# Agent attention and a gated feed-forward: TensorE's loop on 64-row tiles in pairs

## The chip, the cores and the metric

One core of a Trainium2 chip runs the whole problem in one launch. The metric is device time in microseconds (us). Engines are named as the profile names them: PE is TensorE (PEld its weight loads), DVE VectorE, ACT ScalarE, POOL GpSimd, SP SyncE. The L numbers are lines of the kernel before, unless said otherwise.

## The reference

```python
scale = 1.0 / np.sqrt(q.shape[-1])

def sm(a, b):
    s = scale * (a @ b.transpose(0, 2, 1))
    s = s - s.max(-1, keepdims=True)
    e = np.exp(s)
    return e / (e.sum(-1, keepdims=True) + 1e-09)
a2k = sm(agents, k)          # (4, 49, 12480)
agent_v = a2k @ v            # (4, 49, 128)
q2a = sm(q, agents)          # (4, 12480, 49)
x = (q2a @ agent_v).reshape(4 * 12480, 128)
h = x @ w_in                 # w_in 128 x 2048
g = h * (1.0 / (1.0 + np.exp(-1.702 * h)))
out = g @ w_out              # w_out 2048 x 128
```

All arrays are fp32 (w_in and w_out come as float64). There are 4 batches of 12480 tokens, 128 channels and 49 agents.

## The kernel before, in words

Tokens are taken in 52 row groups (13 per batch) of 960, in two halves of 480. F is 2048 wide, in 16 pieces of 128. The product of agent values and `w_in` is folded once per batch into weights of 49 rows, so that the first layer is `q2a` (49 rows by 480 tokens) against 49 x 128 weights. To keep fp32 accuracy with TensorE's rounded fp32 type (`fp32r`), each operand is split into a high and a low part, and a product is a sum of three: high by high, high by low, low by high.

The loop goes in steps of two pieces of F (`two_steps`, 416 of them). The *up* products (`up`, L442 and L445) give `ph`, a PSUM bank of 128 x 480 for each piece and half. The tiles `sa`, `sb` (128 rows) hold the high part, the low part and 30 rows of the third product together, and the 19 rows that are left come as four products on 32-row tiles of the array (`rq` by `wq`, one for each of four banks). ScalarE applies the GELU (`g`, L455). The high part `gh` of `g` is made by a transfer that POOL issues (`gh<-g`, L461), by ScalarE's cast (L465), or once per row group by VectorE; VectorE makes the low part `gl` (L470). The *down* products (L480) add into the two banks of `po`, LAG = 4 pieces behind: `wo_h` by `gh`, `wo_h` by `gl`, `wo_l` by `gh`, each of 128 rows and 480 columns, for either half. When all 16 pieces are in, ScalarE copies both banks out (`store`, L491). `po` has one buffer, `ph` has four.

Between these products lie the jobs of the attention, put at steps by a table (`at`): the query scores of a row group two ahead (48 products of 49 columns in bf16 in two runs, L202), their `Exp` on ScalarE with a table load ahead and one behind (L393), the transposes (L414), and, for the next batch, key scores (L202 too), keys' `Exp` (L285), value products (L300) and weights (L346). The order on PE, ACT, DVE and POOL is that of the code (`manual_schedule`); a queue works in that order.

Of the kernel before, what the change touches and what calls it, by code (L numbers as in the profile page):

```python
# [22 lines left out]
LAG = 4  # L23
G_BUFS = 5
GH_BUFS = 6
GL_BUFS = 4
PAD = 8
Q_AT = 12
E_AT = 0
P_AT = 4  # L30
S_AT = 8
K_AT = 3
V_AT = (6, 11)
V_LAST = 5
R = 30
FIRST_WORDS = 1
FIRST_UP = 2
BOTH = (0,)
ON_DVE = (2,)
# [4 lines left out]
def kernel(  # L44
# [28 lines left out]
    ps_m = ctx.enter_context(tc.tile_pool(name="ps_m", bufs=2, space=bass.MemoryType.PSUM))  # L73
# [11 lines left out]
    for c in range(2):  # L85
        nc.vector.tensor_add(
            out=sel[:, c * H : c * H + A], in0=ident[:, 0:A], in1=ident[:, H : H + A]
        )
        x = c * (R // 2)
        nc.vector.tensor_copy(out=sel[:, c * H + A : (c + 1) * H], in_=sel[:, x : x + R // 2])  # L90

    sel_q = const.tile([P, P], F32, name="sel_q")
    nc.vector.memset(sel_q, 0.0)
    nc.vector.tensor_copy(
        out=sel_q.rearrange("p (i x) -> p i x", i=4)[:, :, 0 : A - R],
        in_=sel[:, R:A].unsqueeze(1).broadcast_to([P, 4, A - R]),
    )

    twice = const.tile([P, 1], F32, name="twice")
    nc.vector.tensor_reduce(  # L100
        out=twice, in_=ident.rearrange("p (c x) -> p c x", c=2)[:, :, A:H], axis=AX.XY, op=ALU.add
    )
    nc.vector.tensor_scalar_mul(out=twice, in0=twice, scalar1=-1.0)
# [91 lines left out]
    def scores(b, parts, ps, c):  # L195
        x0, x1, x2 = parts
        for j in range(c * KB // 2, (c + 1) * KB // 2):
            t = slice(j * TB, j * TB + P)
            o = ps[:, j * A : (j + 1) * A]
            products = [(x0, 0), (x0, 1), (x0, 2), (x1, 0), (x1, 1), (x2, 0)]  # L200
            for i, (x, y) in enumerate(products):
                nc.tensor.matmul(  # L202
                    out=o,
                    lhsT=x[:, t],
                    rhs=ag_part[:, b, y, :],
                    start=(i == 0),
                    stop=(i == len(products) - 1),
                )

    def score_bank():  # L210
        ps = ps_m.tile([P, 512], F32, name="ps_m")
        return ps, ps[:TB, : KB * A].rearrange("p (j a) -> p j a", a=A)
# [7 lines left out]
    def first_key_scores(g, kt):  # L220

        for c in range(2):
            ps = ps_m.tile([P, 512], F32, name="ps_m")
# [11 lines left out]
        running_max(g, score[:TB, g * KB : (g + 1) * KB, :])  # L235

    def running_max(g, s):
        if g == 0:
            nc.vector.tensor_copy(out=run_max[:TB], in_=s)
        else:  # L240
            nc.vector.tensor_tensor(out=run_max[:TB], in0=s, in1=run_max[:TB], op=ALU.max)  # L241

    def key_store(g, s):
        nc.scalar.copy(out=score[:TB, g * KB : (g + 1) * KB, :], in_=s)  # L244
        running_max(g, s)
# [6 lines left out]
    def key_max_1(d):  # L252
        mx = d["mx"]
        ps = ps_m.tile([P, 512], F32, name="ps_m")
# [7 lines left out]
    def key_max_2(d):  # L262
        mrow = d["mrow"]
        ps = ps_m.tile([P, 512], F32, name="ps_m")
        nc.tensor.transpose(out=ps[:TB, :A], in_=mrow[:A], identity=ident[:A, :A])
        nc.vector.tensor_copy(out=max_b[:TB], in_=ps[:TB, :A])
# [31 lines left out]
    def key_matmuls(g, ps, first, last):  # L298
        for j in range(KB):
            nc.tensor.matmul(  # L300
                out=ps[:, : 2 * C + 2],
                lhsT=e_pair[g % 2][:TB, j, :],
                rhs=v_pair[:TB, j, :],
                start=(first and j == 0),
                stop=(last and j == KB - 1),
            )

    def key_values(g):
        ps = ps_m.tile([P, 512], F32, name="ps_m")
        key_matmuls(g, ps, True, True)  # L310
        return ps

    def key_sum(g, ps, acc):
        if g == 0:
            nc.vector.tensor_copy(out=acc, in_=ps[:, : 2 * C + 1])
        else:
            nc.vector.tensor_add(out=acc, in0=ps[:, : 2 * C + 1], in1=acc)


    def weights_0(acc, w):  # L320
        zc = work.tile([P, P], F32, name="zc", bufs=1)
        nc.vector.tensor_copy(out=zc, in_=acc[:, 2 * C : 2 * C + 1].broadcast_to([P, P]))
        w["acc"], w["zc"] = acc, zc

    def weights_1(w, to=sel, name="avT"):
        ps = ps_m.tile([P, 512], F32, name="ps_m")
        nc.tensor.matmul(out=ps[:, 0:P], lhsT=w["acc"][:, 0:C], rhs=to, start=True, stop=False)
        nc.tensor.matmul(out=ps[:, 0:P], lhsT=w["acc"][:, C : 2 * C], rhs=to, start=False, stop=True)
        nc.tensor.matmul(out=ps[:, P : 2 * P], lhsT=w["zc"], rhs=to, start=True, stop=True)
# [3 lines left out]
        avT = work.tile([P, P], F32, name=name, bufs=1)  # L333
        nc.vector.tensor_mul(out=avT, in0=ps[:, 0:P], in1=rz)
        w[name] = avT

    def weights_part(b, w, c):  # L340
        if c == 0:
            wts[b] = wpool.tile([P, F], F32R, name="wh"), wpool.tile([P, F], F32R, name="wq")
        wh, wq = wts[b]
        s = slice(c * 512, (c + 1) * 512)
        pw = ps_m.tile([P, 512], F32, name="ps_m")
        nc.tensor.matmul(out=pw, lhsT=w["avT"], rhs=w_in_sb[:, s], start=True, stop=True)  # L346
        nc.scalar.copy(out=wh[:, s], in_=pw)
        wl = work.tile([P, 512], F32R, name="wl")
        nc.vector.tensor_sub(out=wl[:A], in0=pw[:A], in1=wh[:A, s].bitcast(F32))
        move(wh[A:H, s], wl[0 : R // 2])  # L350
        move(wh[H + A : P, s], wl[R // 2 : R])
        for i in range(4):
            move(wq[i * 32 : i * 32 + A - R, s], wl[R:A])


    def weights_direct(b, w, c):
        if c == 0:
            wts[b] = wpool.tile([P, F], F32R, name="wh"), wpool.tile([P, F], F32R, name="wq")
        wh, wq = wts[b]
        s = slice(c * 512, (c + 1) * 512)  # L360
        pw = ps_m.tile([P, 512], F32, name="ps_m")
        nc.tensor.matmul(out=pw, lhsT=w["avT"], rhs=w_in_sb[:, s], start=True, stop=True)
        hi = work.tile([P, 512], F32R, name="wl")
        nc.scalar.copy(out=hi, in_=pw)
        nc.vector.scalar_tensor_tensor(  # L365
            out=wh[:, s], in0=hi.bitcast(F32), scalar=twice, in1=pw, op0=ALU.mult, op1=ALU.add
        )
        pq = ps_m.tile([P, 512], F32, name="ps_m")
        nc.tensor.matmul(out=pq, lhsT=w["avQ"], rhs=w_in_sb[:, s], start=True, stop=True)
        hi = work.tile([P, 512], F32R, name="wl")  # L370
        nc.scalar.copy(out=hi, in_=pq)
        nc.vector.tensor_sub(out=wq[:, s], in0=pq, in1=hi.bitcast(F32))

    def move(out, in_):
        nc.sync.dma_start(out=out.bitcast(F32), in_=in_.bitcast(F32))
# [7 lines left out]
    def query_shift(s):  # L383
        m = work.tile([P, KB], F32, name="m")
        nc.vector.tensor_reduce(out=m[:TB], in_=s, axis=AX.X, op=ALU.max)
        sd = e_sb[:TB, :, 0:A]
        nc.vector.tensor_tensor(
            out=sd, in0=s, in1=m[:TB].unsqueeze(2).broadcast_to([TB, KB, A]), op=ALU.subtract
# [21 lines left out]
    def query_pairs(g):  # L410
        pp = p_pad
        ps = ps_m.tile([P, 512], F32, name="ps_m")
        for i in range(CH // TB):
            nc.tensor.transpose(  # L414
                out=ps[:, i * TB : (i + 1) * TB], in_=pp[:TB, i, :], identity=ident[:TB, :TB]
            )
        sa = work.tile([P, CH], F32R, name="sa")
        sb = work.tile([P, CH], F32R, name="sb")
        rq = work.tile([P, CH], F32R, name="rq")
        hi = sa[0:A], sb[H : H + A]  # L420
        lo = sa[H : H + A], sb[0:A]
        parts = ps[0:A, :CH], ps[H : H + A, :CH]
        for c in range(2):
            nc.scalar.copy(out=hi[c], in_=parts[c])
        for c, t in enumerate((sa, sb)):
            nc.vector.tensor_sub(out=lo[c], in0=parts[c], in1=hi[c].bitcast(F32))
            move(t[A:H], hi[c][0 : R // 2])
            move(t[H + A : P], hi[c][R // 2 : R])
            for i in (c, c + 2):
                move(rq[i * 32 : i * 32 + A - R], hi[c][R:A])  # L430
        return sa, sb, rq
# [3 lines left out]
    def up(f, wts, pairs):  # L435
        wh, wq = wts
        rq = pairs[2]
        tiles = [(i, c) for i in range(2) for c in range(2)]
        cols = [slice((f + i) * P, (f + i + 1) * P) for i in range(2)]
        ph = [ps_h.tile([P, 512], F32, name="ph") for _ in tiles]  # L440
        for k, (i, c) in enumerate(tiles):
            nc.tensor.matmul(out=ph[k][:, :CH], lhsT=wh[:, cols[i]], rhs=pairs[c], start=True, stop=False)  # L442
        for k, (i, c) in enumerate(tiles):
            r = slice(k * 32, k * 32 + A - R)
            nc.tensor.matmul(  # L445
                out=ph[k][:, :CH],
                lhsT=wq[r, cols[i]],
# [386 lines left out]
```

## Time and profile before

| | us |
|---|---|
| runs, median (lowest to highest of 3) | 2044.2 (2042.5 to 2045.38) |
| span of the profiled execution, first to last instruction | 2042.8 |
| PE busy | 1992.6 |
| DVE busy | 1581.9 |
| ACT busy | 1445.3 |
| POOL busy | 279.2 |

The span is that of one execution under the profiler; its own time isn't listed apart from the runs, the lowest of which lies 0.3 under the span and the highest 2.6 over it. Busy time is the union of an engine's instructions. A product counts as busy to its modelled end, so products that start 0.22 us apart and take 0.38 each leave no idle time; starts say more than ends. In a timeline "x2" on a row merges instructions of one kind that follow each other, and the number in brackets is idle time before the row with what ended it.

### The profile page before, as it was taken

Reading aid. Unit: us, or ns where it says so; the run is one execution under the profiler, and the core shown is the slowest. Engines: PE = TensorE matmul, PEld = TensorE weight load, DVE = VectorE, ACT = ScalarE, POOL = GpSimd, SP = SyncE. Lnnn points to the kernel's source line nnn. Section 1 sums busy time; section 2 is a strip of 40 time slices with the busy share of each in tenths; the row PEclk is TensorE's granted clock in tenths of the full one; section 3 lists DMA queues with packets and bytes.
Section 4 is the critical chain, followed back from the end, with each engine's and each line's share of the span. In section 5 each row is a group of like instructions: output and inputs, shape, how many; then the busy total and the mean of one; then the engine's idle time right before and its main releaser. Section 6 shows DMA issues by size and latency. Waiting matters only on the chain.

```text
span 2042.8 us, 36429 instructions
## 1 busy us (share of the span) xinstructions
PE 1992.6 (98%) x13702; PEld 1524.1 (75%) x13702; DVE 1581.9 (77%) x2038; ACT 1445.3 (71%) x2463; POOL 279.2 (14%) x590
## 2 busy tenths in 40 slices
PE   8779999999999999999999999999999999999999
PEld 7457777777777777777777777777777777777777
DVE  5678888888677879978777878888877776767665
ACT  3357667777776677677676677777777777777775
POOL 3011111111111111111111111111111111111111
PEclk9789999999999999999999999999999999999999
DMA  9545556656455555565555556566545545445443
GB/s 253 155 151 173 178 172 189 177 179 192 157 173 172 185 184 179 179 188 175 171 174 169 181 189 183 172 190 174 170 164 158 179 153 174 156 167 168 161 156 135
DMA packets 128836, 355.13 MB, mean 174 GB/s; under 512 B 15476, under 2 KB 48468, under 8 KB 128660
## 3 DMA queue, kind: packets, MB, share of 16 engines
q0 software_dynamic: 67392, 230.06, 34.5%
q1 hardware_dynamic: 61268, 122.75, 20.8%
q8 instruction: 108, 1.77, 0.4%
q14 instruction: 68, 0.56, 0.1%
HBM read 80.97 MB, written 25.56 MB: 52 GB/s over the span
## 4 chain that ended last, share of the span: by engine, by line
PE 88%; DVE 6%; issue 2%; ACT 2%; DMA 2%; SPq 0%; POOL 0%; ACTq 0%; POOLq 0%; DVEq 0%
PE po L480 52%; PE ph L442 17%; PE ph L445 8%; PE ps_m L202 5%; PE ps_m L300 2%; DVE gl L470 1%; PE ps_m L414 1%; PE ps_m L225 1%; ACT g L455 1%; DVE rest L191 1%; DVE rest L189 1%; DMA gh<-g 1%; PE po L622 1%; PE ps_m L346 0%; DMA words<-w_in 0%
## 5 line engine op out<-in xcount | busy, mean ns | idle before, releaser
L455 ACT ACTIVATE g<-ph 128x480 f32<-128x480 f32 x1664 | 816.8, 577 | 491.3 <-PE ph L445 485.2
L470 DVE TENSOR_TENSOR gl<-g,gh 128x960 fp32r<-128x960 f32 x832 | 941.7, 1153 | 194.8 <-DMA gh<-g 104.7
L480 PE MATMUL po<-gh,wo_h 128*128 128x480 f32 x1664 | 550.7, 412 | 0.0
L480 PE MATMUL po<-gl,wo_h 128*128 128x480 f32 x1664 | 500.8, 382 | 5.3 <-DVE gl L470 4.6
L480 PE MATMUL po<-gh,wo_l 128*128 128x480 f32 x1664 | 499.1, 381 | 0.0
L461 POOL DMA_DIRECT2D gh<-g x468 | 252.1, 539 | 1720.8 <-ACT g L455 1224.5
L480 PEld LDWEIGHTS po<-gl,wo_h 128*128 128x128 f32 x1664 | 310.7, 188 | 63.5 <-DVE gl L470 15.7
L480 PEld LDWEIGHTS po<-gh,wo_l 128*128 128x128 f32 x1664 | 313.1, 188 | 49.6
L480 PEld LDWEIGHTS po<-gh,wo_h 128*128 128x128 f32 x1664 | 272.8, 189 | 82.9 <-issue 64.8
L442 PE MATMUL ph<-sb,wh 128*128 128x480 f32 x832 | 321.1, 386 | 3.2 <-ACT g L455 3.2
L442 PE MATMUL ph<-sa,wh 128*128 128x480 f32 x832 | 319.6, 384 | 2.3 <-DVE wh L365 1.5
L465 ACT CAST gh<-g 128x960 fp32r<-128x960 f32 x312 | 311.7, 999 | 9.0
L445 PE MATMUL ph<-rq,wq 19*128 19x480 f32 x1664 | 204.2, 480 | 0.0
L442 PEld LDWEIGHTS ph<-sb,wh 128*128 128x128 f32 x832 | 156.9, 189 | 38.9 <-ACT g L455 14.8
L442 PEld LDWEIGHTS ph<-sa,wh 128*128 128x128 f32 x832 | 156.8, 189 | 35.2 <-ACT g L455 7.2
L445 PEld LDWEIGHTS ph<-rq,wq 19*128 19x128 f32 x1664 | 79.6, 181 | 136.1 <-issue 136.1
L202 PE MATMUL ps_m<-ag_part,rest 128*128 128x49 bf16 x2184 | 130.4, 184 | 7.8 <-DVE rest L191 7.7
L191 DVE TENSOR_TENSOR rest<-rest 128x480 bf16<-128x480 f32 (+1 forms) x182 | 129.8, 719 | 0.4
L202 PEld LDWEIGHTS <-rest 128*128 128x128 bf16 x2184 | 109.4, 97 | 9.8 <-DVE rest L191 9.4
L241 DVE TENSOR_TENSOR run_max<-ps_m,run_max 120x392 f32<-120x392 f32 x36 | 20.4, 567 | 79.3 <-ACT score L244 79.2
L202 PEld LDWEIGHTS <-qt 128*128 128x128 bf16 x1248 | 61.0, 97 | 24.6 <-issue 24.5
L202 PE MATMUL ps_m<-ag_part,qt 128*128 128x49 bf16 x1248 | 74.3, 186 | 0.0
(116 smaller groups left out, 1345.5 us busy)
## 6 DMA issues: line engine op xcount, KB each, us to landing
gh<-g POOLq DMA_DIRECT2D x468, 480.0 KB, 3.4
kt<-kT SPq DMA_DIRECT2D x52, 480.0 KB
qt<-qT SPq DMA_DIRECT2D x52, 480.0 KB
vt<-v SPq DMA_DIRECT2D x52, 480.0 KB
outT<-o SPq DMA_DIRECT2D x104, 240.0 KB
rq<-sa SPq DMA_DIRECT2D x104, 35.6 KB
rq<-sb SPq DMA_DIRECT2D x104, 35.6 KB
sa<-sa SPq DMA_DIRECT2D x104, 28.1 KB
```

What stands on the lines that cost most here:

```text
L189: nc.vector.tensor_sub(out=r[:, s], in0=t[:, s], in1=halves(t)[0][:, s])
L191: nc.vector.tensor_sub(out=halves(r)[1][:, s], in0=r[:, s], in1=halves(r)[0][:, s])
L202: nc.tensor.matmul(out=o, lhsT=x[:, t], rhs=ag_part[:, b, y, :], start=(i == 0), stop=(i == len(products) - 1),)
L225: nc.tensor.matmul(out=ps[:TB, j * 2 * A : (j + 1) * 2 * A], lhsT=kt[:, c * KB // 2 + j, :], rhs=ag_sb[:, 0:2, :].rearrange("p b a -> p (b ...
L300: nc.tensor.matmul(out=ps[:, : 2 * C + 2], lhsT=e_pair[g % 2][:TB, j, :], rhs=v_pair[:TB, j, :], start=(first and j == 0), stop=(last and ...
L442: nc.tensor.matmul(out=ph[k][:, :CH], lhsT=wh[:, cols[i]], rhs=pairs[c], start=True, stop=False)
L445: nc.tensor.matmul(out=ph[k][:, :CH], lhsT=wq[r, cols[i]], rhs=rq[r], start=False, stop=True, tile_position=(k * 32, 0),)
L455: nc.scalar.activation(out=gs[i][:, c, :], in_=ph[k][:, :CH], func=AF.Gelu_apprx_sigmoid)
L461: nc.gpsimd.dma_start(out=gh, in_=g)
L465: nc.scalar.copy(out=gh, in_=g)
L470: nc.vector.tensor_sub(out=gl, in0=g, in1=gh.bitcast(F32))
L480: nc.tensor.matmul(out=po[c][:, :CH], lhsT=lhsT[:, f, :], rhs=rhs[:, c, :], start=(begin and first), stop=(end and last),)
```

## The change

All products of the loop go onto tiles of 64 rows of the array, in pairs: two products, one on rows 0 to 63 and one on rows 64 to 127, stand next to each other and write different banks.

- *Up*: for one piece of F, three pairs (`wh` by `q_hi`, `wh` by `q_lo`, `wl` by `q_hi`), the upper rows for one half of the tokens and the lower for the other. `sa`, `sb`, `rq`, `wq` and the small transfers that filled their spare rows go; `q_hi`, `q_lo`, `wl` come.
- *Down*: the 128 rows of a piece are two sets of 64. In a first half each row tile adds its rows into one bank of `po` (three pairs), in a second half the row tiles have changed banks (three more pairs). Where the row tile that writes a bank changes, the first product waits for a relay: a `nop` in POOL's queue that itself waits for a product of TensorE that stands behind the bank's last one. The up products of another piece lie between the halves.
- *Order*: the loop goes in gaps (`gap`), 17 for a row group, one with no up products. A gap has jobs, an up step of one piece, the second half of a piece and the first half of the next. LAG is 6. Transfers for `gh` are issued one gap late, at the gap's end; pieces 1 and 9 go by transfer too, and none by VectorE.
- *Scores, value products and transposes* are cut into 64-row pairs as well. The buffers of `ps_m` are one pair of banks in place of two banks. Products with `avT`, and the keys' maximum, stay on 128 rows.
- *Store*: ScalarE copies one bank, VectorE the other.

```diff
-LAG = 4
+LAG = 6
 G_BUFS = 5
-GH_BUFS = 6
-GL_BUFS = 4
+GH_BUFS = 7
+GL_BUFS = 5
...
+    def half_matmul(key, c, **kw):
+        ins = nc.tensor.matmul(tile_position=(c * H, 0), **kw)
+        last = writers.get(key)
+        if last is not None and last[0] != c:
+            while rests[0][0] <= last[1]:
+                rests.pop(0)
+            n, ended, relay = rests[0]
+            if relay is None:
+                relay = rests[0][2] = nc.gpsimd.nop()
+                tc.add_manual_dep(relay.ins, ended.ins.name, behind, reason="bank")
+            tc.add_manual_dep(ins.ins, relay.ins.name, behind, reason="bank")
...
     def up(f, wts, pairs):
-        wh, wq = wts
-        rq = pairs[2]
-        tiles = [(i, c) for i in range(2) for c in range(2)]
-        cols = [slice((f + i) * P, (f + i + 1) * P) for i in range(2)]
-        ph = [ps_h.tile([P, 512], F32, name="ph") for _ in tiles]
-        for k, (i, c) in enumerate(tiles):
-            nc.tensor.matmul(out=ph[k][:, :CH], lhsT=wh[:, cols[i]], rhs=pairs[c], start=True, stop=False)
...
+        products = [(wh, q_hi), (wh, q_lo), (wl, q_hi)]
+        for k, (w, q) in enumerate(products):
+            for c in range(2):
+                r = slice(c * H, c * H + A)
+                half_matmul(
+                    ph[c].name,
+                    c,
+                    out=ph[c][:, :CH],
+                    lhsT=w[r, cols],
+                    rhs=q[r],
...
+    def down(f, gh, gl, po, swap, begin, end):
+        products = [(wo_h, gh), (wo_h, gl), (wo_l, gh)]
+        for i, (w, x) in enumerate(products):
+            for c in range(2):
+                to = c ^ swap
+                r = slice(c * H, (c + 1) * H)
+                half_matmul(
+                    po[to].name,
...
     def store(b, g, po):
         for c in range(2):
             o = work.tile([P, CH], F32, name="o", tag="o")
-            nc.scalar.copy(out=o, in_=po[c][:, :CH])
+            if c == 0:
+                nc.scalar.copy(out=o, in_=po[c][:, :CH])
+            else:
+                nc.vector.tensor_copy(out=o, in_=po[c][:, :CH])
...
+        before, late[:] = list(late), []
+        rest()
         for job in at.pop(t, ()):
             job()
...
+        if u is not None:
+            if u < steps:
+                do_up(u)
+                rest()
+            do_low(u - 3)
         if t >= LAG:
...
+            do_downs(n, k)
+        for u in before:
+            do_high(u)
+
+    def do_downs(n, k):
+        if k == 0:
+            po[n] = [ps_o.tile([P, 512], F32, name=f"po{c}") for c in range(2)]
+        first_whole = NF - LAG - 1 if n == B * NG - 1 else NF
+        if 0 < k <= first_whole:
+            do_down(n, k - 1, True)
+        if k < first_whole:
+            do_down(n, k, False)
+        elif k < NF:
+            do_down_whole(n, k)
+        else:
+            store(*divmod(n, NG), po.pop(n))
```

The order of instructions shows it at three places. First TensorE in the middle of a row group; this is one step before (in brackets what an instruction waits for):

```order
L442 MATMUL ph<-sa,wh 128x480 [waits Activation_49]
L442 MATMUL ph<-sb,wh 128x480 [waits Activation_49]
L442 MATMUL ph<-sa,wh 128x480 [waits Activation_49]
L442 MATMUL ph<-sb,wh 128x480 [waits Activation_49]
L445 MATMUL ph<-rq,wq 128x480 x4
L480 MATMUL po_12946<-gh,wo_h 128x480
L480 MATMUL po_12947<-gh,wo_h 128x480
L480 MATMUL po_12946<-gl,wo_h 128x480 [waits DVE_49]
L480 MATMUL po_12947<-gl,wo_h 128x480
L480 MATMUL po_12946<-gh,wo_l 128x480
L480 MATMUL po_12947<-gh,wo_l 128x480
```

And this is TensorE in one gap of the change (lines of the changed kernel; `Pool_sequencer` is the relay):

```order
L192 MATMUL ph<-q_hi,wh 128x480 [waits Activation_49] x2
L192 MATMUL ph<-q_lo,wh 128x480 x2
L192 MATMUL ph<-q_hi,wl 128x480 x2
L192 MATMUL po_13879<-gh,wo_h 128x480 [waits Pool_sequencer_49]
L192 MATMUL po_13878<-gh,wo_h 128x480
L192 MATMUL po_13879<-gl,wo_h 128x480
L192 MATMUL po_13878<-gl,wo_h 128x480
L192 MATMUL po_13879<-gh,wo_l 128x480
L192 MATMUL po_13878<-gh,wo_l 128x480
L192 MATMUL po_13879<-gh,wo_h 128x480
L192 MATMUL po_13878<-gh,wo_h 128x480
L192 MATMUL po_13879<-gl,wo_h 128x480 [waits DVE_49]
```

The four-fold 32-row products are gone, an up step has six products of one piece, and the second half of a piece (its first row waits for the relay) is followed by the first half of the next. There are 915 such waits in the program, 825 of them at down products.

The second place is ScalarE from the end of a row group to the `Exp` of the next, before:

```order
L393 ACT_TABLE_LOAD
L393 ACTIVATE e_sb<-e_sb 120x8x49
L455 ACT_TABLE_LOAD
L455 ACTIVATE g<-ph 128x480 x4
L491 COPY o<-po_6721 128x480
L491 COPY o<-po_6722 128x480
L455 ACTIVATE g<-ph 128x480 x4
L424 CAST sa<-ps_m 49x480
```

And in the change:

```order
L480 ACTIVATE g<-ph 128x480 x4
L491 CAST gh<-g 128x960
L526 COPY o<-po_2682 128x480
L480 ACTIVATE g<-ph 128x480 x4
L491 CAST gh<-g 128x960
L480 ACTIVATE g<-ph 128x480 x2
L406 ACT_TABLE_LOAD
L406 ACTIVATE e_sb<-e_sb 120x8x49
L480 ACT_TABLE_LOAD
L480 ACTIVATE g<-ph 128x480 x4
```

The `Exp` and its tables have moved from ahead of the copies to behind them, four gaps into the row group, and the copy now stands behind a cast of `gh`.

The third place is TensorE at the first down products of a row group, before:

```order
L414 MATMUL ps_m<-ident,p_pad 128x120 [waits DVE_49,PE_49]
L414 MATMUL ps_m<-ident,p_pad 128x120 x3
L480 MATMUL po_3205<-gh,wo_h 128x480 [waits DMASW4_49,Activation_49]
L480 MATMUL po_3206<-gh,wo_h 128x480 [waits Activation_49]
L480 MATMUL po_3205<-gl,wo_h 128x480 [waits DVE_49]
```

And in the change, where the run of 24 score pairs and one up step stand ahead of them:

```order
L192 LDWEIGHTS rest
L192 MATMUL ps_m<-ag_part,rest 128x49
L192 MATMUL ph<-q_hi,wh 128x480 [waits Activation_49] x2
L192 MATMUL ph<-q_lo,wh 128x480 x2
L192 MATMUL ph<-q_hi,wl 128x480 x2
L192 MATMUL po_14583<-gh,wo_h 128x480 [waits DMASW4_49,Activation_49]
L192 MATMUL po_14584<-gh,wo_h 128x480 [waits DVE_49]
L192 MATMUL po_14583<-gl,wo_h 128x480
```

Either bank now waits for its own copy, on ScalarE or on VectorE, and what stands ahead of the wait is other work.

## Rows read from the trace of the kernel before

**Rows 1.** The page: busy time and shares, and the chain that ended last.

```profile
PE 1992.6 (98%) x13702; PEld 1524.1 (75%) x13702; DVE 1581.9 (77%) x2038; ACT 1445.3 (71%) x2463; POOL 279.2 (14%) x590
...
PE 88%; DVE 6%; issue 2%; ACT 2%; DMA 2%; SPq 0%; POOL 0%; ACTq 0%; POOLq 0%; DVEq 0%
```

**Rows 2.** Windows by stretch: busy us of each engine, granted clock, DMA.

```profile
core 0: us, PE busy (x) PEld busy (x) DVE busy (x) ACT busy (x) POOL busy (x), PEclk, DMA share, GB/s
...
800.00:1200.00 400.00, 397.46 (x2716) 302.04 (x2715) 324.07 (x418) 291.99 (x496) 52.59 (x114) 1.00 0.57 179
```

**Rows 3.** Waits of TensorE's weight loads: us in total, times, longest.

```profile
PEld ph L445 <- issue: 136.1, 415, 0.4
PEld po L480 <- issue: 64.8, 279, 0.5
PEld L202 <- issue: 42.9, 179, 0.4
PEld ph L442 <- ACT g L455: 22.0, 68, 3.5
PEld po L480 <- DVE gl L470: 15.7, 35, 3.5
```

**Rows 4.** Timeline, one step and the quiet end: start us, us.

```profile
999.77 0.38 PE L442 MATMUL ph<-sb,wh 128*128 128x480 f32 x1
...
1003.64 0.39 PE L442 MATMUL ph<-sa,wh 128*128 128x480 f32 x1
1003.64 0.19 PEld L442 LDWEIGHTS ph<-sb,wh 128*128 128x128 f32 x1
1003.87 0.38 PE L442 MATMUL ph<-sb,wh 128*128 128x480 f32 x1
...
1004.31 0.38 PE L442 MATMUL ph<-sb,wh 128*128 128x480 f32 x1
1004.61 0.19 PEld L445 LDWEIGHTS ph<-rq,wq 19*128 19x128 f32 x4 [0.33 <-issue]
1004.61 0.49 PE L445 MATMUL ph<-rq,wq 19*128 19x480 f32 x4
1005.03 0.30 PEld L480 LDWEIGHTS po<-gh,wo_h 128*128 128x128 f32 x2 [0.23 <-issue]
1005.03 0.70 PE L480 MATMUL po<-gh,wo_h 128*128 128x480 f32 x2
1005.13 1.03 ACT L455 ACTIVATE g<-ph 128x480 f32<-128x480 f32 x2 [1.10 <-PE ph L445]
1005.36 0.40 PEld L480 LDWEIGHTS po<-gl,wo_h 128*128 128x128 f32 x2
...
2033.23 0.60 PE L480 MATMUL po<-gh,wo_h 128*128 128x480 f32 x2
2033.67 0.60 PE L480 MATMUL po<-gl,wo_h 128*128 128x480 f32 x2
```

**Rows 5.** Timeline, a run of 24 score products and the down products behind.

```profile
1010.11 0.25 PE L202 MATMUL ps_m<-ag_part,qt 128*128 128x49 bf16 x3
...
1010.73 0.68 PE L480 MATMUL po<-gh,wo_h 128*128 128x480 f32 x2
...
1011.25 0.59 PE L480 MATMUL po<-gl,wo_h 128*128 128x480 f32 x2
```

**Rows 6.** Timeline of ScalarE: a cast, the exponentials and the store.

```profile
1007.12 1.00 ACT L465 CAST gh<-g 128x960 fp32r<-128x960 f32 x1
...
1021.72 1.28 ACT L393 ACT_TABLE_LOAD   x1
...
1023.45 0.51 ACT L285 ACTIVATE score<-score 120x392 f32<-120x392 f32 x1
1023.99 1.28 ACT L455 ACT_TABLE_LOAD   x1
1025.28 1.96 ACT L455 ACTIVATE g<-ph 128x480 f32<-128x480 f32 x4
1027.10 1.05 ACT L491 COPY o<-po 128x480 f32<-128x480 f32 x2
```

**Rows 7.** Timeline of POOL: the issue of a transfer.

```profile
1006.46 0.53 POOL L461 DMA_DIRECT2D gh<-g  x1 [3.57 <-DVE gl L470]
```

**Rows 8.** Groups by line: products of the second set of weights.

```profile
L369 PE MATMUL ps_m<-w_in_sb,avQ 128*128 128x512 f32 x8 | 6.3, 886 | 0.0
```

More of the change, by code (lines that the diff above doesn't have):

```diff
@@ L88 @@
         )
[L89 to L103, printed above, removed]
     e_pair = []
@@ L332, in weights_1, with weights_parts @@
         nc.vector.reciprocal(out=rz, in_=rz)
-        avT = work.tile([P, P], F32, name=name, bufs=1)
+        avT = work.tile([P, P], F32, name="avT", bufs=1)
         nc.vector.tensor_mul(out=avT, in0=ps[:, 0:P], in1=rz)
-        w[name] = avT
-    def weights_part(b, w, c):
+        w["avT"] = avT
+    def weights_parts(b, w, c):
         if c == 0:
[L342 to L353, printed above, removed]
@@ L356, in weights_direct @@
[L356 to L372, printed above, removed]
@@ new lines, in query_pairs @@
+        ps = two_banks()
+        q_hi = work.tile([P, CH], F32R, name="q_hi")
+        q_lo = work.tile([P, CH], F32R, name="q_lo")
+        r = slice(0, H + A)
+        rows = [slice(0, H), slice(H, TB)]
+        for i in range(CH // TB):
+            for c, t in enumerate(rows):
+                n = t.stop - t.start
+                half_matmul(
+                    (ps.name, c),
+                    c,
+                    out=ps[:, c, i * n : (i + 1) * n],
+                    lhsT=pp[t, i, :],
+                    rhs=ident[t, t],
+                    start=True,
+                    stop=True,
+                    is_transpose=True,
+                )
@@ new lines, in piece, with scored @@
+        def piece(q, c):
+            t = rows[c]
+            return q[r].rearrange("p (i t) -> p i t", t=TB)[:, :, t]
+        def scored(c):
+            n = rows[c].stop - rows[c].start
+            return ps[r, c, : CH // TB * n].rearrange("p (i t) -> p i t", t=n)
+        for c in range(2):
+            nc.scalar.copy(out=piece(q_hi, c), in_=scored(c))
+        for c in range(2):
+            nc.vector.tensor_sub(out=piece(q_lo, c), in0=scored(c), in1=piece(q_hi, c).bitcast(F32))
+        return q_hi, q_lo
@@ L507 @@
     pairs = {}
+    exps = {}
     def do_key_load(b, g):
@@ L639 @@
     weights_1(w0)
-    weights_1(w0, sel_q, "avQ")
-    for c in range(2):
-        if c:
-            up_weights(c, words_in[c])
-        weights_direct(0, w0, c)
-    for i in range(4):
-        do_query_split(1, i)
-    ahead(1)
-    do_query_softmax(1)
+    up_weights(1, words_in[1])
+    weights_parts(0, w0, 0)
     down_weights(0, words[0])
     steps = B * NG * NF
-    per_batch = NG * NF
+    gaps = LAG + B * NG * GAPS
     at = {}
-    pe_steps = {n * NF + f for n in range(B * NG) for f in (Q_AT, Q_AT + 1, P_AT)}
+    busy = set()
@@ L657, in put, with gap_of, take, free @@
+    def gap_of(u):
+        if u < LAG:
+            return u
+        n, k = divmod(u - LAG, NF)
+        return LAG + n * GAPS + (k + 1 if k else 0)
     def put(t, fn):
         at.setdefault(t, []).append(fn)
-    def pe_step(t):
-        while t in pe_steps:
+    def take(t, runs):
+        assert not busy.intersection(range(t, t + runs)), t
+        busy.update(range(t, t + runs + 1))
+    def free(t):
+        while t in busy or t + 1 in busy:
             t += 1
-        pe_steps.add(t)
+        take(t, 1)
@@ L738, with do_high, do_up, do_low @@
     po = {}
-    def jobs(t):
+    late = []
+    def do_high(u):
+        gh[u] = high(u % NF, g[u])
+    def do_up(u):
+        n, f = divmod(u, NF)
+        g[u] = up(f, wts[n // NG], pairs[n])
+        if by_dma(f):
+            late.append(u)
+        else:
+            do_high(u)
+        if f == NF - 1:
+            pairs.pop(n)
+    def do_low(u):
+        if 0 <= u < steps:
+            gl[u] = low(g.pop(u), gh[u])
+    def do_down(n, f, second):
+        u = n * NF + f
+        down(f, gh[u], gl[u], po[n], (f + second) % 2, f == 0 and not second, f == NF - 1 and second)
+        if second:
+            gh.pop(u), gl.pop(u)
@@ L792 @@
     with tc.manual_schedule(engines={E.PE, E.Activation, E.DVE, E.Pool}):
-        for t in range(0, steps + LAG, 2):
-            two_steps(t)
-    assert not at
+        for t in range(gaps):
+            gap(t)
+    assert not at, sorted(at)
 _INS = ["qT", "kT", "v", "agT", "w_in", "w_out"]
```

399 lines of the change are left out of this document (196 added, 203 removed).

## The prediction

> **What bounds the kernel now.** I read the shares of busy time first: TensorE is busy 98% of the span, and the chain that ended last lies on it for 88% [rows 1]. That alone doesn't say that its products are the limit, since a product counts as busy until its modelled end. So next the stretches: from 800 to 1200 us TensorE is busy nearly throughout at a granted clock of 1.00 (2.4 GHz), VectorE for 324 of 400 us and ScalarE for 292 [rows 2]. Both have room, VectorE not much. Then the waits: the longest on TensorE's weight loads have no releaser ("issue"): 136.1 us ahead of the 19-row products, 64.8 ahead of the first product for `po`, 42.9 ahead of the scores; next to them 22.0 for ScalarE's GELU and 15.7 for VectorE's low part [rows 3]. The timeline shows what "issue" is. The four up products start some 0.22 apart; then nothing starts for 0.30 us, until four 19-row loads and products start together (1004.31 to 1004.61); the next 128-row product starts 0.42 later, and its load stands open before the second one goes (1005.03 to 1005.36) [rows 4]. These are the passages from 128-row to 32-row tiles and back. They cost TensorE idle time in every step, so the stage is bound by TensorE with two drains in it.
>
> **The change, part by part.** All sums go against the span of 2042.8 us; the runs' median, 2044.2, is 1.4 above it.
>
> *Up products.* A step of two groups of F takes 4.10 us from one second up product to the next (999.77 to 1003.87) and holds 16 full products besides the 19-row four [rows 4]. The new step holds no passage: 3 pairs up and 6 pairs down for each group, 18 pairs in two. What a pair of 64-row products takes is in no row. Nearest are the full products, 0.22 apart (two in 0.44 even at the end, where other engines are idle), and the four 19-row ones, which start together [rows 4]. So I take one pair for one product, 0.218: 3.92 us, 0.18 less, times 416 steps: **-75 us**. Bounds: 480 columns at 2.4 GHz are 0.200, with 0.003 between starts 0.203, so 7488 pairs could take 112 us less still; weights that load one tile after the other (0.11 each, below) would make a pair 0.222, 30 more.
>
> *Scores.* Before, a run of 24 score products takes 0.62 us (1010.11 to 1010.73) [rows 5]; now 24 pairs. As pairs they cost the same; one after the other 0.62 more per run, 113 us for the 182 runs of 91 groups. The 19-row four start together, so I stand near the low end, +0.1 per run for loads that wait in order: **+18**. Behind a run the load of the first full product is open (0.52 for two products, 1010.73 to 1011.25, in place of 0.44) [rows 5]. Before, one of the two runs stood where a drain had just been paid; now both runs, and the transposes too, stand between 480-column products: 143 x 0.085 = **+12**.
>
> *The store.* `po` has one buffer, so the first down product of a row group waits until both copies of the group before are done. On ScalarE the copy now stands behind the GELU of that gap and the cast of `gh` behind it. I count from the gap's start: the third up pair starts at 0.44 and ends at 0.82 (0.38 long), the GELU starts 0.03 later and takes 1.03 [rows 4], the cast 1.00 and the copy 0.55 [rows 6]: 3.5. TensorE has up (0.65) and the second half (0.65), then in the next gap scores (0.71) and up (0.65): 2.66. So it waits 0.84, where before both copies followed straight on the GELU (1027.10 to 1028.15 [rows 6]) and no wait for them is among the long ones [rows 3]. 51 x 0.84 = **+43**. Bounds: nothing, if scores slower than pairs fill the time; 0.9 per group. VectorE's copy of the other half is done earlier by the same count.
>
> *The exponentials.* Two table loads and the query's `Exp` take 3.05 us (1021.72 to 1025.28, less the 0.51 for the keys) [rows 6]. They now stand ahead of a single GELU whose `ph` buffers are wanted two gaps, 3.92 us, later, and whose transfer's issue stands in POOL's queue ahead of a relay. GELU ends at 3.05 + 1.03 = 4.08: `up` waits 0.2. Issue starts 0.30 after the GELU and takes 0.53 (1006.16, 1006.46) [rows 4, 7], so the relay behind it runs at about 5.0, while TensorE comes to its wait at 4.77: 0.25 more. In 21 of the 51 groups the keys' `Exp` adds about 0.8: 1.3 in all. 30 x 0.45 + 21 x 1.3 = 41; of the 22.0 that is there now [rows 3] nothing else is left, so **+19**. Bounds: -22 to +40.
>
> *The relay elsewhere.* Queued behind its wait on TensorE are the second half's six products and all that follows. The product that it waits for ends 0.38 after its start; POOL and TensorE answer in 0.03 to 0.30 each (1005.10 to 1005.13 on ScalarE, 0.30 at POOL) [rows 4, 7]: 0.44 to 0.98. The last pair's own 0.22 and three up pairs, 0.65, hide 0.87. The upper end is a transfer's preparation, which a relay doesn't need; I take it as hidden: **0**. Without the up products it would cost 0.2 to 0.7 per gap.
>
> *Smaller parts.* The keys' maximum and the weights still run on 128 rows: 15 places with a passage either way, 0.4 each: **+6**. The start loses the second set of weight products (6.3 us of TensorE for `avQ` [rows 8]), but VectorE still converts the same words: **-6**, between -12 and 0. A lag of six groups in place of four should spare part of VectorE's 15.7: **-8**, between -15 and +10, as VectorE keeps its work in a shorter time.
>
> Sum: -75 + 18 + 12 + 43 + 19 + 6 - 6 - 8 = +9, or **2052 us**: the drains that go are given back in waits on ScalarE.
>
> A rule that bears on the pairs: the Trainium skill, "TensorE: Matmul & The Clock Gate", Part 3, § The mechanism, says that a weight load overlaps a running product only where its row group differs. The rows show otherwise: a 128-row load starts with the product on the same rows (both at 1003.64) and the next product follows 0.23 later [rows 4]. By the rule each tile's next load would stand open; what that gives is a rival below.
>
> **The rivals.** *A pair is faster than a full product.* It decides soon: 9 us over 7488 pairs is 1.2 ns, so below some 0.217 per pair the sum is under the time before. Toward 0.203 to 0.212 it gives 1940 to 2010. For it: nothing shows that the 0.018 beyond 480 columns belongs to 64-row tiles. Against: the same 0.22 in the quiet end [rows 4] speaks for a pace of the operand's stream, not of a neighbour.
>
> *The new waits don't come.* If ScalarE is far enough ahead, store and exponentials give 62 us less: 1990. For it: ScalarE is idle 27% of the time [rows 2]. Against: it works in order, and the chain of GELU, cast and copy starts only when its up products end.
>
> *Scores one by one.* +95 on the sum, less some 31 that fall into the wait for the store: 2115. For it: two instructions with a load per 49 columns; against: the 19-row four.
>
> *The relay shows in every gap.* If POOL and TensorE take 0.2 more than hidden, 832 x 0.2 = 166: 2220. It decides from an answer over 0.49 in all. For it: POOL's 0.30; against: that is a transfer's.
>
> *Loads open in each tile.* A first load after a drain takes some 0.11 (1005.03 to the second product's turn; four of them overlap) [rows 4]; 7488 x 0.11 = 800: 2850. Against: the load at 1003.64. It is the case that the Trainium skill's rule, cited above from "TensorE: Matmul & The Clock Gate", would have.
>
> **How the numbers follow.** Given back, 2025 to 2085: 0.48 (of it 0.10 faster, 0.08 the same, 0.30 slower). Faster pairs: 0.15. No new waits: 0.15 (0.14 faster, 0.01 the same). Scores singly: 0.13. Relay: 0.06. Open loads: 0.03. Faster by over 0.2% (which is about what a measurement of this kernel can tell from no change): 0.39, within 0.2% 0.09, slower 0.52. The range leaves out the fastest pairs, half of that case (0.08), the last two rivals and the top of the scores (0.12): 1965 to 2130. The likeliest case alone has 2025 to 2085.
>
> **What would show it.** Right: no idle TensorE with "issue" between up and down; pairs that start within 0.01 us of each other and 0.22 apart; at each first down product of a row group about 0.8 us of waiting on ScalarE's copy, and some two gaps after each `Exp` a wait on GELU or POOL. ScalarE's casts and VectorE's low parts as long as before. Wrong: a pair interval away from 0.22 in either direction (it weighs most: 10 ns are 75 us), score runs much over 0.7 us, relays that TensorE waits for in ordinary gaps, or no wait at the store.

## The result and the profile after

The changed kernel takes 2023.9 us (median of 4 runs, 2021.6 to 2026.6), the kernel before on the same chip 2043.4 (2042.2 to 2045.4): a ratio of 0.9905, with a 95% interval of 0.9891 to 0.9919. The forecast was 2052, slower by 0.4%; it became faster by 0.95%. The time lies inside the range given, the direction was wrong. The profiled execution has a span of 2024.8 us, 18.0 under that of before; it is the slowest of the four, and by the medians the change gives 19.5.

The page after, busy time and chain, answers to [rows 1]:

```profile
PE 1953.1 (96%) x25158; PEld 1771.6 (87%) x25158; DVE 1553.4 (77%) x2025; ACT 1404.0 (69%) x2407; POOL 303.4 (15%) x642
...
PE 80%; ACT 8%; DVE 4%; issue 4%; DMA 3%; SPq 0%; POOL 0%; ACTq 0%; DVEq 0%; POOLq 0%
```

TensorE has nearly twice the instructions and is still what the chain lies on, but ScalarE's share of the chain went from 2% to 8%. The waits of TensorE's weight loads, against [rows 3] (us in total, times, longest; L526 is ScalarE's copy of `po`, L528 VectorE's, L480 the GELU, L199 the relay):

```profile
PEld po L192 <- ACT o L526: 36.7, 46, 1.5
PEld L192 <- issue: 34.2, 134, 4.3
PEld ph L192 <- ACT g L480: 29.1, 63, 1.1
...
PEld po L192 <- DVE o L528: 6.1, 11, 1.6
...
PEld po L192 <- POOLq L199: 4.1, 4, 1.7
```

The 136.1 us and 64.8 us of "issue" around the 19-row products are gone; the 34.2 that are left stand ahead of the scores, where 42.9 stood. In their place TensorE waits for ScalarE: for its copy of `po` in 46 of 51 row groups, and for the GELU 29.1 us against 22.0. The relay shows 4 times in the whole program. No wait on VectorE's low part is among the long ones any more (15.7 before).

The timeline of TensorE in a plain gap, up pairs and a second half, against [rows 4]:

```profile
1785.19 0.57 PE L192 MATMUL ph<-q_hi,wh 49*128 49x480 f32 x2
1785.41 0.57 PE L192 MATMUL ph<-q_lo,wh 49*128 49x480 f32 x2
1785.63 0.57 PE L192 MATMUL ph<-q_hi,wl 49*128 49x480 f32 x2
1785.84 0.58 PE L192 MATMUL po<-gh,wo_h 64*128 64x480 f32 x2
1786.06 0.58 PE L192 MATMUL po<-gl,wo_h 64*128 64x480 f32 x2
1786.28 0.57 PE L192 MATMUL po<-gh,wo_l 64*128 64x480 f32 x2
```

A row is a pair. Pairs start 0.22 us apart, across the change of banks too (1785.63 to 1785.84), as single 128-row products did. But a pair lasts 0.57 where one product lasts 0.38: its two products start up to 0.2 us after each other.

The sums of the trace's starts of TensorE products, each start counted to the next one, give the balance. From the GELU of the second row group's first piece (at 140.4 us before, 134.9 after) to the last product, before and after:

| us | forecast, whole program | measured |
|---|---|---|
| plain steps and gaps: 408 x 4.119 (median of 207 steps) to 816 x 1.963 (median of 423 gaps) | -75 | -79 |
| stretches of scores, transposes and value products: 179.4 to 190.3 | +18 | +11 |
| 128-row products of weights and maximum: 8.1 to 15.4 | +6 | +7 |
| up and down stretches beyond their plain length, where all waits lie: 29.2 to 77.8 | 43 + 19 + 12 - 8 = +66 | +49 |
| up to the second row group: 140.4 to 134.9 | -6 | -5.5 |
| sum | +9 | -17.5 |

What the change takes away was sized well, what is given back was not. ScalarE around a row group's end shows the store:

```profile
1786.04 1.03 ACT L480 ACTIVATE g<-ph 128x480 f32<-128x480 f32 x2 [0.92 <-PE ph L192]
1787.10 1.00 ACT L491 CAST gh<-g 128x960 fp32r<-128x960 f32 x1
1788.00 0.55 ACT L526 COPY o<-po 128x480 f32<-128x480 f32 x1
```

And TensorE there, from the end of the scores (the [ ] is idle time with what ended it):

```profile
1787.24 0.46 PE L192 MATMUL ph<-q_hi,wh 49*128 49x480 f32 x1
1787.25 0.23 PE L192 MATMUL ps_m<-ag_part,rest 64*128 64x49 bf16 x3
1787.32 0.46 PE L192 MATMUL ph<-q_hi,wh 49*128 49x480 f32 x1
1787.55 0.45 PE L192 MATMUL ph<-q_lo,wh 49*128 49x480 f32 x2
1787.76 0.46 PE L192 MATMUL ph<-q_hi,wl 49*128 49x480 f32 x2
1788.61 0.48 PE L192 MATMUL po<-gh,wo_h 64*128 64x480 f32 x2 [0.39 <-ACT o L526]
1788.93 0.38 PE L192 MATMUL po<-gl,wo_h 64*128 64x480 f32 x2
```

The copy stands behind GELU and cast as forecast, and the first down product waits for its end (1788.55). But the gap began at 1785.19: the copy ends 3.36 later, not 3.5 (the forecast's own addends make 3.43), since it starts 0.90 after the start of a cast of 1.00; and TensorE could go on at 1788.0 (1787.76 and 0.22), 2.8 later, not 2.66, since the load behind the scores is open. 0.6 us are lost, not 0.84.

### The profile page after: what moved, and what is told of

Read it like the earlier page. It is cut to its first block, busy times and chain, and to the rows that moved or that the text cites. A ratio compares the mean times of both kernels' runs of the same rounds, so it can differ in the third digit from the quotient of the medians.

```text
span 2024.8 us, 59521 instructions
## 1 busy us (share of the span) xinstructions
PE 1953.1 (96%) x25158; PEld 1771.6 (87%) x25158; DVE 1553.4 (77%) x2025; ACT 1404.0 (69%) x2407; POOL 303.4 (15%) x642
## 3 DMA queue, kind: packets, MB, share of 16 engines
q1 hardware_dynamic: 49188, 106.55, 19.5%
## 4 chain that ended last, share of the span: by engine, by line
PE 80%; ACT 8%; DVE 4%; issue 4%; DMA 3%; SPq 0%; POOL 0%; ACTq 0%; DVEq 0%; POOLq 0%
PE po L192 46%; PE ph L192 24%; PE ps_m L192 7%; ACT g L480 3%; DMA gh<-g 2%; ACT L480 1%; DVE gl L496 1%; ACT L406 1%; PE ph L261 1%; ACT o L526 1%; PE ps_m L383 1%; ACT score L321 1%; DVE rest L173 0%; PE po L657 0%; PE po L518 0%
## 5 line engine op out<-in xcount | busy, mean ns | idle before, releaser
L480 ACT ACTIVATE g<-ph 128x480 f32<-128x480 f32 x1664 | 850.8, 570 | 474.3 <-PE ph L192 469.4
L192 PE MATMUL po<-gh,wo_h 64*128 64x480 f32 x3300 | 799.0, 383 | 23.1 <-ACT o L526 18.1
L192 PE MATMUL po<-gl,wo_h 64*128 64x480 f32 x3300 | 789.0, 378 | 0.0
L192 PE MATMUL po<-gh,wo_l 64*128 64x480 f32 x3300 | 787.3, 377 | 0.0
L192 PEld LDWEIGHTS po<-gh,wo_h 64*128 64x128 f32 x3300 | 460.2, 185 | 62.7 <-ACT o L526 36.7
L192 PEld LDWEIGHTS po<-gh,wo_l 64*128 64x128 f32 x3300 | 461.9, 185 | 19.7
L192 PEld LDWEIGHTS po<-gl,wo_h 64*128 64x128 f32 x3300 | 463.2, 186 | 17.0
L192 PE MATMUL ph<-q_hi,wh 49*128 49x480 f32 x1664 | 431.8, 406 | 9.1 <-ACT g L480 8.3
L192 PE MATMUL ph<-q_lo,wh 49*128 49x480 f32 x1664 | 405.6, 380 | 0.0
L192 PE MATMUL ph<-q_hi,wl 49*128 49x480 f32 x1664 | 402.1, 379 | 0.0
L192 PEld LDWEIGHTS ph<-q_hi,wh 49*128 49x128 f32 x1664 | 237.5, 186 | 44.6 <-ACT g L480 29.1
L192 PEld LDWEIGHTS ph<-q_hi,wl 49*128 49x128 f32 x1664 | 237.6, 186 | 9.9 <-DVE wl L387 0.2
```

The lines of the kernel that those rows point to most:

```text
L192: ins = nc.tensor.matmul(tile_position=(c * H, 0), **kw)
L480: nc.scalar.activation(out=g[:, c, :], in_=ph[c][:, :CH], func=AF.Gelu_apprx_sigmoid)
```

## The experiments

The theory after the comparison (A in most runs): every mechanism of the forecast is there, but the waits on ScalarE are smaller than it made them. The rivals: the waits are only passed on from one releaser to the next, or what was gained is not the passages.

**The store, with piece 5 by transfer.**

```diff
-BY_DMA = (1, 9)
+BY_DMA = (1, 5, 9)
```

> Piece 5 of every row group has its high part made by the transfer instead of ScalarE's cast, so that ScalarE's copy of po follows straight on the GELU. Theory A (the wait at the store is what the cast ahead of the copy makes, some 0.55 us in each of the 36 row groups where VectorE's copy is done early): the copy ends 1.0 us earlier, some 0.3 before TensorE wants the bank, and the time falls by 20 to 28 us, to 1996 to 2004 us. Rival B (the wait is only passed on, to VectorE's copy of the other bank or to piece 5's transfer and its low part): 2016 to 2028 us, with as long a wait on another releaser at the first down products.

Measured: 1998.1 us, ratio 0.9773 (0.9758 to 0.9787).

**The store, with the copy ahead of the cast:**

```diff
...
+        elif f == LAG - 1 and n:
+            casts.append(u)
         else:
             do_high(u)
...
             do_downs(n, k)
+        while casts:
+            do_high(casts.pop())
```

> ScalarE's copy of po is issued ahead of the cast of piece 5 instead of behind it; nothing else is changed, and no transfer is added. Theory A: the same gain as with piece 5 by transfer, 20 to 28 us, to 1996 to 2004 us, less a little if the cast, now 0.55 us later, is late for its low part. Rival B: the wait is passed on, 2016 to 2028 us. If this run gains and the other doesn't, the added transfer costs what it gives.

Measured: 1996.5 us, ratio 0.9762 (0.9746 to 0.9779). Both give the same, so the cast ahead of the copy is the cause: 27 us by order alone. In the waits of the second run ScalarE's copy shows once (0.5 us), and VectorE's copy of the other bank has come forward, from 6.1 us in 11 groups to:

```profile
PEld ph L192 <- ACT g L480: 28.2, 63, 1.1
PEld po L192 <- DVE o L528: 11.8, 19, 2.3
```

So a part of the wait was indeed passed on, a small one.

**VectorE's copy ahead of its low part**, on top of the last one:

```diff
-            do_low(u - 3)
+            if not casts:
+                do_low(u - 3)
         if t >= LAG:
             do_downs(n, k)
+        if casts:
+            do_low(u - 3)
```

> As the run with the copy ahead of the cast, and in the same gap VectorE's copy of the other bank is issued ahead of its low part (1.15 us) instead of behind it. That run still shows 7.4 us of waiting for VectorE's copy in 19 row groups, and 2.9 of open loads behind. Theory A (VectorE is behind in its queue in the row groups with key splits, and the low part can wait): 5 to 9 us less than with the copy alone ahead, 1987 to 1992 us. Rival B (the low part is then late for its own down products): 1995 us or more, with waits on the low part.

Measured: 1983.3 us, ratio 0.9701 (0.9687 to 0.9716): 13 less than the copy alone, more than the 5 to 9 expected. By the sums of starts 7 of it lie in the up and down stretches (the copy) and 6 in the scores' stretches, which I had not expected. These 6 lie in the length of the score runs: 131 us in sum in the changed kernel, 135 with the copy alone ahead, 129 here. So 4 of them give back what the copy alone had cost there; why the length moves isn't shown. The store in all: 41 us.

**The exponentials left out of the changed kernel:**

```diff
-        put(t + E_AT, lambda m=m: do_query_exp(m))
...
-        put(slot, lambda ks=ks: key_exp(ks[0], len(ks)))
+        pass
```

> The loop's Exp instructions, of queries and keys, are left out with their table loads, so the softmax weights of the loop are not computed. Theory A (the waits behind the exponentials are some 20 us of GELU and some 3 us of relays): 1996 to 2006 us. Rival B (ScalarE's 3.05 us also delay casts, low parts and copies that TensorE waits for elsewhere): under 1990 us. Rival C (the tables are hidden and the waits on the GELU come from the full GELU queue alone): 2018 to 2026 us.

Measured: 1999.6 us, ratio 0.9782 (0.9768 to 0.9797): 24 less. The wait on ScalarE's copy has grown from 36.7 to 42.2, so the 24 are net. The wait on the GELU has gone from 29.1 to:

```profile
PEld ph L192 <- ACT g L480: 2.2, 5, 1.1
```

**The same, left out of the kernel before:**

> The kernel before, with the loop's Exp instructions and their table loads left out (the softmax weights are not computed), as in the run of the changed kernel without them, which is 24 us under the changed kernel. The price of the exponentials before the change is the other side of the term. Theory A (my term: 22 us of waits on the GELU before, all from the exponentials): 18 to 24 us less, 2020 to 2026 us, so that the change left this price as it was. Rival B (before the change they were hidden for the most part): 2034 to 2044 us, so that the change made them dearer by 15 us or more.

Measured: 2030.0 us, ratio 0.993 (0.9916 to 0.9945): 15 less. There the wait on the GELU (22.0 in [rows 3]) has gone to:

```profile
PEld ph L442 <- ACT g L455: 6.1, 6, 3.5
```

So 6.1 of the 22.0 were not the exponentials'. They cost 15 us before and 24 after, 9 more. Each of these times is known to some 3 us, but the sums of starts agree: the gaps and steps behind the tables are 24 us beyond their plain length after the change and 14 before. Both theories had put this too far out, A at no difference and B at 15 or more.

**The relay without cover: the second half ahead of the up products.**

```diff
+        if t >= LAG:
+            do_second(n, k)
+            rest()
         if u is not None:
             if u < steps:
                 do_up(u)
-                rest()
...
```

> The second half of a piece stands ahead of the up products instead of behind them, so that in a gap without other jobs nothing covers the relay. The traces give 0.38 us for the last product to end, 0.04 to the relay, some 0.05 back: 0.47 against a next start after 0.03 to 0.19, and an open weight load of 0.11. Theory A (the up products between the halves hide the relay): 0.25 to 0.4 us in each of some 780 gaps, 2220 to 2340 us. Rival B (the relay answers while the pairs drain, and the cover isn't needed): under 2080 us.

Measured: 2276.6 us (one run), 253 more than the changed kernel. The waits of its weight loads have the relay first:

```profile
PEld po L192 <- POOLq L199: 330.5, 594, 1.6
```

And its timeline of TensorE at the end of a first half:

```profile
1797.27 0.40 PE L192 MATMUL po<-gh,wo_l 64*128 64x480 f32 x2
1797.78 0.49 PE L192 MATMUL po<-gh,wo_h 64*128 64x480 f32 x2
1798.10 0.38 PE L192 MATMUL po<-gl,wo_h 64*128 64x480 f32 x2
```

The second half starts 0.51 after the last pair in place of 0.22, and its first pair takes 0.32 in place of 0.22 for the open load: 0.39 in a gap without cover, 0.30 a gap on the mean (253 / 832). In the changed kernel the three up pairs between the halves hide all of it but the 4 waits (4.1 us) in the list above.

**The down products back on 128 rows, the up products in pairs:**

```diff
-        first_whole = NF - LAG - 1 if n == B * NG - 1 else NF
+        first_whole = 0
...
```

> The down products go back to 128 rows (six for each piece, no relay); the up products stay in pairs on 64-row tiles. Theory A (TensorE drains at each passage between tilings, which was the cost that the change took away): two passages per gap of 0.09 us drain and 0.11 us open load, 0.2 each as before around the 19-row products, so 832 x 0.4 = 330 us more, less what then hides in the wait at the store: 2260 to 2370 us. Rival B (only 32-row tiles cost a passage; 64-row and 128-row products follow each other freely): 2000 to 2060 us.

Measured: 2313.2 us (one run), 289 more. Its timeline of TensorE over one gap (L518 are the whole down products):

```profile
1795.59 0.48 PE L192 MATMUL ph<-q_hi,wh 49*128 49x480 f32 x2
...
1796.44 0.71 PE L518 MATMUL po<-gh,wo_h 128*128 128x480 f32 x2
...
1797.95 0.49 PE L192 MATMUL ph<-q_hi,wh 49*128 49x480 f32 x2
```

The waits of its weight loads without a releaser are back too:

```profile
PEld po L518 <- issue: 243.9, 724, 0.6
PEld ph L192 <- ACT g L480: 159.7, 468, 1.8
```

The second row is no wait of its own kind: the first up product starts 0.31 after the last whole one by the median, whether the list names the GELU or "issue".

Three up pairs take 0.85 (0.65 without a passage), six whole products 1.51 (1.31): 0.2 at each change of tiling, 0.40 a gap, 333 in 832 gaps, of which some 40 hide in other waits. A passage between 64 and 128 rows thus costs what one between 128 and 32 did. The Trainium skill has it on the page "TensorEngine Tiling (Array Packing)", section Key Properties: a change of the tiling mode drains the engine. The trace agrees, with 0.2 us for each.

**The scores back on 128 rows**, 24 products a run:

```diff
-                for c in range(2):
-                    bank = c ^ run
...
+                nc.tensor.matmul(
+                    out=ps[:, run, j * A : (j + 1) * A],
+                    lhsT=x[:, t : t + P],
+                    rhs=ag_part[:, b, y, :],
```

> The scores of queries and keys go back to 128 rows, 24 products a run, one bank a run, without relays. Theory A (a run of pairs costs what a run of products costs, and a passage costs 0.2 either way): 182 runs x 0.4 less 0.1 for the slower run of pairs, some 30 to 60 us more, less what hides in the wait at the store: 2035 to 2085 us. Rival B (short products hide the passage, so the pairs of scores gave nothing): 2010 to 2028 us.

Measured: 2043.1 us, ratio 1.000 (0.9990 to 1.0009), 19 more than the changed kernel. By the median over its runs the first score starts 0.31 after the product ahead (0.20 with pairs), and the next product 0.11 behind the last score (0.025): 0.2 a run, 36 in 182. The run itself is 0.04 shorter (8), and the rest hides. The waits of the scores' loads without a releaser, 34.2 in the changed kernel, are:

```profile
PEld L215 <- issue: 64.8, 179, 4.3
```

So scores as pairs are worth the whole gain of the change, because they avoid the passages, not because they are faster.

**The kernel before without its 19-row products** (shortened; the products ahead of them end the sum):

```diff
-            nc.tensor.matmul(out=ph[k][:, :CH], lhsT=wh[:, cols[i]], rhs=pairs[c], start=True, stop=False)
-        for k, (i, c) in enumerate(tiles):
-            r = slice(k * 32, k * 32 + A - R)
...
+            nc.tensor.matmul(out=ph[k][:, :CH], lhsT=wh[:, cols[i]], rhs=pairs[c], start=True, stop=True)
```

> The kernel before, with its 19-row products left out (so part of the third product of the first layer is not added); everything else stays, the loop then has no passage from one tiling to another. Theory A (four 19-row products and their two passages take 0.61 of a step of 4.10 us, the rest is 16 products of 0.218): 416 x 0.61 = 254 us less, 1790 us, up to 1850 where VectorE (1582 us busy) doesn't keep up. Rival B (the idle time ahead of the 19-row products only stands in for another wait): over 1900 us.

Measured: 1848.8 us (one run), at the upper end. A plain step takes 3.47 us in its trace (1600.01 to 1603.47), the 16 products of 0.217 that the forecast counted. Most of the rest is VectorE, busy 355 of 400 us in this window (columns as in [rows 2]):

```profile
800.00:1200.00 400.00, 392.45 (x2788) 321.77 (x2787) 355.28 (x460) 322.31 (x550) 59.54 (x131) 1.00 0.61 197
```

and waited for, as the waits of the weight loads have it:

```profile
PEld po L469 <- DVE gl L459: 50.4, 85, 4.2
```

**LAG of four again:**

```diff
-LAG = 6
+LAG = 4
-GH_BUFS = 7
-GL_BUFS = 5
+GH_BUFS = 6
+GL_BUFS = 4
...
-BY_DMA = (1, 9)
+BY_DMA = (7, 15)
```

> LAG is 4 again, with the buffers of gh and gl as before (6 and 4); the pieces that go by transfer besides the even ones are shifted with it (7 and 15), so that they stand at the same gaps. Theory A (the lag of six is what took away the 15.7 us that TensorE waited for VectorE's low part): some 8 to 20 us more, 2030 to 2046 us, with waits on the low part again. Rival B (those waits came from the order of the kernel before, and one piece per gap is what ended them): 2018 to 2030 us.

Measured: 2277.0 us, ratio 1.1143 (1.1126 to 1.1159), 253 more: the mechanism of A, at more than ten times its price. The waits of its weight loads:

```profile
PEld po L192 <- DVE gl L496: 284.2, 257, 5.7
```

And one of them in the timeline of TensorE:

```profile
1782.03 0.39 PE L192 MATMUL po<-gh,wo_h 64*128 64x480 f32 x2
1783.38 0.48 PE L192 MATMUL po<-gl,wo_h 64*128 64x480 f32 x2 [0.96 <-DVE gl L496]
```

From the end of a piece's GELU to the end of its low part the changed kernel takes 4.9 to 7.7 us (medians by piece: the transfer goes out a gap late and takes 3.2, the low part 1.15, the rest is queueing on VectorE). Between the GELU's end and the first product that wants it lie LAG - 1 gaps less some 0.4 us: 5.5 us for four, 9.4 for six. In this order the larger lag is a condition, not a small gain. The buffers were changed with it, so how much is theirs isn't told apart.

**A version that beats both: the second value run 7 gaps later**, on top of both store copies ahead:

```diff
-V_AT = (6, 10)
+V_AT = (6, 17)
```

> As the run before it, and the second of the two runs of value products of a row group stands 7 gaps later, at the gap at which the next row group's exponentials stand, so that TensorE has 1 us more work while ScalarE is behind. Theory A (what TensorE waits for behind the exponentials, 17 us, nearly all in the 23 row groups that have keys' Exp too, is ScalarE's 3.56 us against two gaps of 3.93): some 10 to 14 us less than the run before it, 1974 to 1981 us. Rival B (the wait returns behind the value products, or VectorE's sum of the values is late for the scores): within 4 us of the run before it.

Measured: 1963.2 us, ratio 0.9598 (0.9582 to 0.9614): 20 less than the run before it, 60.7 less than the changed kernel. The wait on the GELU goes from 28.8 to:

```profile
PEld ph L192 <- ACT g L480: 13.0, 28, 1.8
```

By the sums of starts 13 of the 20 lie in the up and down stretches, as A has it: behind the exponentials with keys' `Exp` 18 us become 2. (These are 21 row groups; the 23 of the expectation is a miscount.) The other 7 lie in the stretches of scores and value products, which I haven't followed.

## Why the prediction was wrong, step by step

**The step that failed** is the size of the two waits on ScalarE, "51 x 0.84 = +43" and "30 x 0.45 + 21 x 1.3 = 41; of the 22.0 that is there now [...] +19". For the first, the sums of starts show 28 us of waiting for ScalarE's copy (0.6 in 46 groups), and the run with the copy ahead of the cast gives 27. For the second they show 24 us after the change and 14 before, 10 more (9 by the runs without exponentials). With 38 in place of 62 the sum is -15, not +9: these two sizes alone turn its sign.

That -15 lies near the measured -18.0 is in part luck, since other terms missed too and nearly cancel. VectorE's copy and the open load behind the wait, which the store's term put at nothing, cost 11, so that the store in all cost 39 by the sums of starts, not far from its 43. Against that, the scores' stretches came out 7 under their term, the plain gaps 4, and what is left of the up and down stretches (12 - 8 in the forecast) 4.

*The store.* 0.6 a group, in 46 groups. Three things were miscounted. The sum to the copy's end was written as 3.5 where its addends make 3.43. The copy starts 0.90 after the start of a cast of 1.00, so the two overlap by 0.1 us. The Trainium skill has this for activations, on the page "ScalarE: Activation LUTs", section What ACT_TABLE_LOAD costs, with some 93 ns for back-to-back ones, and the trace agrees, here for a copy behind a cast. And the open load behind the scores, which I booked as a term of its own (+12), is in 51 of its 143 places time that TensorE spends anyway while the copy is under way: it was counted as a cost and not as cover. The sentence on VectorE's copy ("done earlier by the same count") was wrong in 11 of the 57 waits at these products, and in 19 row groups once ScalarE's copy is out of the way. With it and the open load the first three down pairs of a row group take 11 us beyond their plain length in sum; 1 is left of it where VectorE's copy goes ahead too.

*The exponentials.* The row after the tables is as forecast: `up` waits 0.15 in plain row groups (0.2 forecast; the up step at 1799.25 takes 0.81 in place of 0.65). In the 21 groups with keys' `Exp` it is some 0.8 (18 us in the sums of starts), not 1.3. Before the change the steps behind the tables lost 14 us, not the 22.0 that I took off: part of that wait was not the exponentials', and a wait of the weight loads is not all lost. The relay behind the issue of a transfer didn't show. The timeline of POOL behind an `Exp`:

```profile
1799.75 0.53 POOL L489 DMA_DIRECT2D gh<-g  x1 [3.04 <-DVE z L411]
```

And of TensorE there:

```profile
1799.25 0.74 PE L192 MATMUL ph<-q_hi,wh 49*128 49x480 f32 x2
1799.51 0.69 PE L192 MATMUL ph<-q_lo,wh 49*128 49x480 f32 x2
1799.83 0.59 PE L192 MATMUL ph<-q_hi,wl 49*128 49x480 f32 x2
1800.06 0.59 PE L192 MATMUL po<-gh,wo_h 64*128 64x480 f32 x2
```

The second half, whose relay stands behind this issue in POOL's queue, starts at 1800.06, before the issue's 0.53 us are over (1800.28). The relay itself is recorded at 1799.74, 0.01 ahead of the issue's start. At 40 more issues a relay is recorded 0.01 to 0.02 ahead of the start, and at 3 some 0.15 into the issue. A relay waits for the start of an issue, not for its end; I had added the whole of it, 0.25 in 51 groups, 13 us.

*The rest.* A pair for one product of 0.218 was right (a plain gap of nine pairs takes 1.963); the -75 came out as -79 since a plain step before takes 4.119, not 4.10. "Faster pairs" and "loads open in each tile" are refuted by the same cadence. Scores as pairs cost 0.64 a run by the median from the first start to the last, +0.04, in place of +0.1. The relay is hidden as counted: cover 0.87 against 0.51, now measured without cover. The start came out as forecast, the 128-row products too. The low part's -8 had the sign, as its wait (15.7 before) is gone, but the run with the lag of four shows what that rested on: the lag, or its buffers. "The new waits don't come" is refuted as well: they came, at 38 in place of 62, with 11 more on VectorE's side. Of what the forecast named as signs, the pairs that start within 0.01 us of each other are wrong (up to 0.2 apart, with the same cadence), and there is no wait on POOL behind an `Exp`.

## What to carry to other kernels

A sum of a large gain and several given-back waits has its sign in the waits: count the cover of each on both engines to 0.1 us, with the overlap between instructions of the waiting engine's queue, and don't book a delay as a cost where it only fills a wait that is booked too. When a one-buffer accumulator is emptied, put the copies first in their engines' queues: two such swaps gave 41 us, twice what the whole rewrite did. Keep a stretch on one tiling of TensorE: each change of row tiling cost 0.2 us in the runs, for long and short products alike, and two products on 64-row tiles took the time of one.

## What the runs showed of the hardware that was not expected

The two row tiles of a pair go each at their own pace. After the scores the first up product of one tile starts at 1787.24, before three score products of the other tile that stand ahead of it in TensorE's order (1787.25, in the rows above). The distance between the tiles, anything from 0 to 0.2 us, stays for many gaps until a wait brings them together (0.2 in all eleven gaps from 1765.7 to 1785.6), and leaves the cadence of long pairs at 0.218; a run of scores takes 0.74 when the tiles come apart (1786.50 to 1787.24) and 0.63 after a wait has brought them together (1789.37 to 1790.00). A relay of POOL passes a transfer's issue that is still shown as running, as told above.
